# Scaling the softmax rows on DVE instead of ACT, and putting the transposes first in a group of attention's PE work

## The chip, the cores and the metric

The kernel runs on one core of a Trainium2 chip. The metric is the time of one execution in device microseconds (us); the time before is the median of three runs, and the change is judged against it. The engines are PE (TensorE: matmuls, and the transposes that are made of matmuls), DVE (VectorE), ACT (ScalarE), POOL (GpSimd) and SP (SyncE, which here only issues transfers).

## The reference

```python
# q, k, v: (8 batches, 8 heads, 576 rows, 64)
scores = q @ k.T / 8 + slope[h] * -(i - j)       # only 0 <= i - j < 128, else -1e9
attn   = softmax(scores)                         # sum + 1e-9 in the denominator
x      = (attn @ v) -> (4608 tokens, 512)
h      = max(x @ w1, x @ w2, x @ w3)             # 512 -> 768
out    = h @ w_out                               # 768 -> 512
```

Attention has a causal window of 128, so a block of 128 query rows needs only its own and the preceding block of 128 keys. 576 rows are four blocks of 128 and one of 64.

## The kernel before, in words

**Attention** goes by tasks (batch, pair of heads): 32 tasks of five blocks, 160 steps in all. One step is one block of both heads.

- `products` computes scores for two steps at a time into PSUM (`ps_s`, or `ps_m` in batch 0), with 64x64 tiles of PE.
- `score` merges the two key blocks into one by a predicated copy (L329, L332), adds the bias and takes the maximum on DVE (L344), and takes the exponential on ACT (L348). The result is the tile `p`, 128 rows by two heads by 128, and a row sum in `st`.
- `sums_of` adds 1e-9 and takes the reciprocal on DVE (L357, L360), for two steps or one.
- `normalise` multiplies `p` by that reciprocal, one value per row: L367, once for each step and head, 320 times in all.
- `turn` transposes `p` for two steps on PE (L376, four transposes into the tile `pt`), copies `pt` to SBUF on ACT (L380, L386, L389), and POOL cuts it into the two triangles of the window (L390, L394), the tile `pp`.
- `mix` multiplies `pp` by `v` (L416) into `ps_x`, with column tiles of 64; the last block has 64x64 tiles. ACT copies the finished `ps_x` to `xk` (L425).

**The three-way maximum and the output product** are split into high and low parts (L442 on ACT, L443 on DVE) and multiplied in 128x128x288 matmuls with three products for each pair of parts. Batch 0 uses the plain weights (`plain_unit`, L585); batches 1 to 7 use a seven-product scheme on 2x2 blocks (`unit`, L623). The results are taken from three PSUM buffers (`ps_m0` to `ps_m2`) by DVE and ACT (`put`, L533 to L552, and L632).

**Weights** are made during batch 0 (L132 to L176: fetched by SP, decoded on ACT and DVE, split) and recombined during batch 1 (`add`, `add_part`, L183 to L205). From batch 2 on they are streamed from DRAM by transfers that POOL issues (L270), into a ring of two buffers.

**What sets the order.** `at(when, ...)` enters each piece of work with a time in steps; the list is sorted, and so the program order comes about. Attention of step s enters at s (shifted by 2 and 4 steps from batch 1 and 2 on); the matmul units are spread evenly between the ends of the attention of successive batches. So PE's work alternates: a run of 128x128x288 matmuls, and then a group of attention's work. Such a group is entered at one even step c: mix at c + 0.001, products at c + 0.002, turn at c + 0.003 (turn belongs to the pair that began four steps earlier, mix to the pair six steps earlier). A scheduler at compile time sets the fixed order of each engine's queue; from batch 2's seventh step on PE keeps the program order as written (`keep_in_program_order`).

Each engine takes its instructions strictly in its queue's order. An instruction of DVE that has to wait holds up all behind it.

Of the kernel before, what the change touches and what calls it, by code (L numbers as in the profile page):

```python
# [12 lines left out]
AF = mybir.ActivationFunctionType  # L13
ALU = mybir.AluOpType
# [4 lines left out]
LAG_T, LAG_X = 4, 6  # L19
# [10 lines left out]
def attention_maxout_kernel(  # L30
# [11 lines left out]
    nc = tc.nc  # L42
# [7 lines left out]
    NB = (S + P - 1) // P  # L50
# [35 lines left out]
        out=prev, in_=prev, pattern=[[1, P]], compare_op=ALU.is_gt, fill=0.0,  # L86
# [275 lines left out]
    def normalise(t, i):  # L362
        n = rows[i]
        st, two = stats[t, i // 2]
        for a, p in enumerate(two):
            for j in range(2):
                nc.scalar.activation(p[:n, j], p[:n, j], AF.Copy, scale=st[:n, 2, a, j:j + 1])  # L367

    def turn(s):
        pt = ps_t.tile([P, 2, 2, P], F32, name="pt")  # L370
# [270 lines left out]
    def at(when, what, *args):  # L641
        events.append((when, len(events), what, args))
# [3 lines left out]
    for t, (b, hp) in enumerate(tasks):  # L646
        for i in range(NB):
            s = t * NB + i + shift[b]
            if i == LOAD_I and t + 2 < len(tasks):
                at(s - 0.4, load, t + 2)  # L650
            if i == NB - 1 and t + 1 < len(tasks):
                at(s - 0.4, load_v, t + 1)
            if i == 0 and 0 < t < NP:
                at(s - 1, slopes, t)
            c = s - (t * NB + i) % 2

            if s == c:
                at(c + 0.002, products, t * NB + i)
                at(c + LAG_T + 0.003, turn, t * NB + i)
            at(s + 0.04, score, t, i)  # L660
            if i % 2 or i + 1 == NB:
                at(s + 0.9, sums_of, t, i)
                at(s + 1.3, normalise, t, i)
            e = t * NB + next(min(e + 1, NB - 1) for e in GROUPS if e >= i)
            at(e - e % 2 + shift[b] + LAG_X + 0.001, mix, t, i)
# [78 lines left out]
```

## Time and profile before

| | |
|---|---|
| median of 3 runs (lowest to highest) | 802.09 us (800.0 to 804.02) |
| the profiled execution's own time | 799.82 us |
| its span, from first to last instruction | 797.7 us |
| PE busy | 759.2 us (95%) |
| DVE busy | 559.9 us (70%) |
| ACT busy | 531.3 us (67%) |
| POOL busy | 166.8 us (21%) |
| mean granted TensorE clock | 0.964 |

The span stands 2.1 us below its own execution's time, and this execution 2.3 us below the median.

How to read it: a span of an engine is busy or idle, and for idle time the profile names what ended it (its releaser). The trace falls into four stages. Until 75 us there is only the attention of batch 0, with the first part of the weights' preparation. From 75 to 160 us the plain products of batch 0 run beside the attention of batch 1. From 160 to 300 us batch 1 runs with the recombined weights being made, and from 300 to 700 us the same pattern repeats for the later batches. After 700 us there is no attention left.

### The profile page before, as it was taken

The page shows a single profiled execution, that of the slowest core. Times are in us where ns is not written, and L with a number is a line of the kernel's source. Part 1 is how long each engine was busy: PE and PEld are TensorE (multiplying, and loading weights), DVE is VectorE, ACT ScalarE, POOL GpSimd, SP SyncE. Part 2 cuts the span into 40 slices and gives each one's busy share as a digit, 9 for nine tenths or more (in the row PEclk, how much of TensorE's full clock was granted, in tenths as well). Part 3 has the DMA queues.
Part 4 walks back from the last instruction along what each step waited for, and adds up shares of the span by engine and source line. Part 5 has one row for each costly group of instructions (what it writes and reads, how often), then busy time and mean ns, then how long its engine had stood idle before and what let it go on. Part 6 is the DMA issues. An engine that isn't in the chain of part 4 may idle for free.

```text
span 797.7 us, 18112 instructions
## 1 busy us (share of the span) xinstructions
PE 759.2 (95%) x6344; PEld 674.2 (85%) x6344; DVE 559.9 (70%) x1897; ACT 531.3 (67%) x1736; POOL 166.8 (21%) x374
## 2 busy tenths in 40 slices
PE   4776998999999999999999999999999999999987
PEld 2434987998888998899989999898988999899987
DVE  5677888488999757793777747793777747673662
ACT  6888888568878656775667657676667667552332
POOL 1221111111214122221223122221222122201100
PEclk7756999999999999999999999999999999999999
DMA  8775785387899459864887459864788458755951
GB/s 282 266 243 171 228 302 208 115 297 231 318 329 314 166 196 320 286 215 138 285 295 252 162 187 323 282 234 136 277 285 257 160 195 288 245 198 195 301 181 60
DMA packets 53771, 187.96 MB, mean 236 GB/s; under 512 B 5936, under 2 KB 14896, under 8 KB 46768
## 3 DMA queue, kind: packets, MB, share of 16 engines
q0 software_dynamic: 15552, 99.10, 37.6%
q1 hardware_dynamic: 37984, 87.64, 32.0%
q8 instruction: 50, 0.82, 0.4%
q14 instruction: 41, 0.34, 0.1%
q10 hardware_dynamic: 144, 0.07, 0.0%
HBM read 154.53 MB, written 32.24 MB: 234 GB/s over the span
## 4 chain that ended last, share of the span: by engine, by line
PE 65%; DVE 12%; issue 9%; ACT 6%; DMA 4%; POOL 2%; SPq 0%; POOLq 0%; ACTq 0%; DVEq 0%
PE ps_m L623 44%; PE ps_x L416 6%; PE ps_m L585 6%; PE ps_s L314 5%; PE pt L376 4%; DMA wt<-keep 2%; ACT p L348 2%; DVE hs L443 2%; DVE xs L443 2%; DMA hs<-in_w_all 1%; DVE t L549 1%; DVE s L344 1%; DVE ps_s L332 1%; DVE hq L550 1%; ACT xs L442 1%
## 5 line engine op out<-in xcount | busy, mean ns | idle before, releaser
L623 PE MATMUL ps_m<-xs,wt 128*128 128x288 f32 x2646 | 370.4, 297 | 4.1 <-DMA wt<-keep 1.7
L623 PEld LDWEIGHTS ps_m<-xs,wt 128*128 128x128 f32 x2646 | 355.4, 188 | 7.9 <-DVE t L549 3.8
L390 POOL TENSOR_SCALAR_AFFINE_SELECT pp<-pr 128x256 f32<-128x256 f32 (+1 forms) x128 | 54.7, 428 | 401.9 <-ACT pr L389 220.2
L348 ACT ACTIVATE p<-s,st 128x128 f32<-128x128 f32 (+1 forms) x320 | 127.0, 399 | 16.0 <-DVE st L344 14.6
L632 ACT COPY t<-ps_m 128x288 f32<-128x288 f32 x231 | 89.7, 394 | 71.2 <-PE ps_m L623 70.8
L623 PE MATMUL ps_m<-hs,ow 128*128 128x288 f32 x882 | 124.0, 297 | 1.6 <-DVE hs L443 0.8
L367 ACT ACTIVATE p<-p,st 128x128 f32<-128x128 f32 (+1 forms) x320 | 110.5, 396 | 19.4 <-DVE st L360 19.4
L623 PEld LDWEIGHTS ps_m<-hs,ow 128*128 128x128 f32 x882 | 118.7, 188 | 3.1 <-ACT t L632 1.2
L270 POOL DMA_DIRECT2D wt<-keep x108 | 58.3, 539 | 194.3 <-PE ps_m L623 187.7
L344 DVE CUSTOM_DVE_ANT_0 s<-ps_s,bias 128x128 f32<-128x128 f32 (+1 forms) x300 | 76.7, 281 | 17.4 <-PE ps_s L314 13.6
L416 PE MATMUL ps_x<-pp,v 128*64 128x256 f32 (+3 forms) x768 | 81.3, 339 | 3.7 <-POOL pp L390 3.6
L332 DVE COPY_PREDICATED ps_s<-prev,ps_s 128x256 f32<-128x256 uint8 x120 | 50.8, 423 | 46.2 <-PE ps_s L314 44.7
L549 DVE TENSOR_TENSOR t<-ps_m,t 128x288 f32<-128x288 f32 x126 | 56.5, 452 | 36.3 <-PE ps_m L623 24.2
L314 PE MATMUL ps_s<-qk 64*64 64x192 f32 (+1 forms) x1080 | 70.2, 336 | 9.2 <-DVE st L344 5.0
L416 PEld LDWEIGHTS ps_x<-pp,v 128*64 128x64 f32 (+1 forms) x768 | 46.1, 142 | 29.9 <-issue 10.6
L442 ACT CAST hs<-hq 128x288 fp32r<-128x288 f32 x117 | 49.0, 430 | 31.9 <-DVE hq L550 16.5
L376 PE MATMUL pt<-ident,p 128*128 128x128 f32 (+1 forms) x320 | 59.2, 296 | 11.2 <-ACT p L367 7.1
L376 PEld LDWEIGHTS pt<-ident,p 128*128 128x128 f32 (+1 forms) x320 | 34.8, 146 | 40.3 <-issue 18.9
L585 PE MATMUL ps_m<-xs,wt 128*128 128x288 f32 x432 | 63.3, 306 | 3.3 <-DVE xs L443 2.6
L585 PEld LDWEIGHTS ps_m<-xs,wt 128*128 128x128 f32 x432 | 60.6, 196 | 4.2 <-DVE xs L443 3.0
L314 PEld LDWEIGHTS ps_s<-qk 64*64 64x64 f32 x1080 | 41.1, 138 | 26.7 <-issue 10.5
L389 ACT COPY pr<-pt 128x256 f32<-128x256 f32 x64 | 18.9, 321 | 66.5 <-PE pt L376 66.5
(58 smaller groups left out, 849.4 us busy)
## 6 DMA issues: line engine op xcount, KB each, us to landing
wt<-keep POOLq DMA_DIRECT2D x54, 1024.0 KB, 7.3
wt<-keep POOLq DMA_DIRECT2D x54, 768.0 KB, 5.5
qk<-in_qk SPq DMA_DIRECT2D x31, 576.0 KB, 5.8
hs<-in_w_all SPq DMA_DIRECT2D x24, 512.0 KB, 5.0
v<-in_v SPq DMA_DIRECT2D x32, 320.0 KB, 4.6
keep<-wt SPq DMA_DIRECT2D x36, 256.0 KB, 3.8
outT<-t SPq DMA_DIRECT2D x64, 144.0 KB, 1.8
wt<-keep SPq DMA_DIRECT2D x27, 256.0 KB, 4.2
```

Of the source, the lines that this page charges most:

```text
L270: nc.gpsimd.dma_start(wts[n, a], keep[n % 9][a])
L314: pe(nc.tensor.matmul(ps[j][d:d + D, o:o + k1 - k0], lhsT=qkt[t][j * D:(j + 1) * D, 0, q0:q0 + D], rhs=qkt[t][j * D:(j + 1) * D, 1, k0:k1] ...
L332: nc.vector.copy_predicated(both[:, :, P:], mask.unsqueeze(1).broadcast_to([n, 2, P]), both[:, :, :P],)
L344: nc.vector.tensor_tensor_reduce(out=s[:n], in0=ps[j][:n, P:2 * P], in1=(bias if i else bias0)[:n, 2 * hp + j, :], scale=-0.125, scalar=3. ...
L348: nc.scalar.activation(p[:n, j], s[:n], AF.Exp, bias=st[:n, 0, a, j:j + 1], scale=-1.0, accum_out=st[:n, 1, a, j:j + 1])
L367: nc.scalar.activation(p[:n, j], p[:n, j], AF.Copy, scale=st[:n, 2, a, j:j + 1])
L376: pe(nc.tensor.transpose(out=pt[:, a, j, :n], in_=p[:n, j], identity=ident[:n, :n]))
L416: pe(nc.tensor.matmul(x[j * D:(j + 1) * D, c:c + e - a], lhsT=vv[:n, i, j * D:(j + 1) * D], rhs=w[:n, j].rearrange("p a b -> p (a b)")[:, ...
L549: nc.vector.tensor_tensor(out=s, in0=ps, in1=e, op=ALU.add)
L585: pe(nc.tensor.matmul(ps, lhsT=lt, rhs=rt, start=m == 0 and c == 0, stop=m == len(pairs) - 1, skip_group_check=True,))
L623: pe(nc.tensor.matmul(ps, lhsT=lt, rhs=rt, start=i == 0 and k in (0, 1, 4), stop=i == len(pairs) - 1, skip_group_check=True,))
L632: nc.scalar.copy(out=e, in_=ps)
```

## The change

Two edits. `normalise` issues its multiplication as a DVE `tensor_scalar` with the reciprocal as a per-partition scalar, where it was an ACT `activation` with `Copy` and that scale. And `turn` is entered at c + 0.000 where it was at c + 0.003, so that it stands ahead of mix and products of the same group.

```diff
@@ normalise
         for a, p in enumerate(two):
             for j in range(2):
-                nc.scalar.activation(p[:n, j], p[:n, j], AF.Copy, scale=st[:n, 2, a, j:j + 1])
+                nc.vector.tensor_scalar(
+                    out=p[:n, j], in0=p[:n, j], scalar1=st[:n, 2, a, j:j + 1], scalar2=None, op0=ALU.mult
+                )
@@ the list of events
             if s == c:
                 at(c + 0.002, products, t * NB + i)
-                at(c + LAG_T + 0.003, turn, t * NB + i)
+                at(c + LAG_T, turn, t * NB + i)
```

Lines of the changed kernel from L368 on have numbers two higher (transposes L378, mix L418, splits L444 and L445, units L625).

What that does to the queues, at three places. The first is PE's queue in the repeating pattern of the later batches; `pt` is written by transposes, `ps_s` by score products, `ps_x` by mix, `ps_m` by the 288-wide matmuls. Before:

```order
L623 MATMUL ps_m_5883<-xs,wt_5729 128x288 x6
L416 MATMUL ps_x<-pp,v 64x256 x4
L314 MATMUL ps_s<-qk 64x192 x6
L376 MATMUL pt<-ident,p 128x64 x2
L376 MATMUL pt<-ident,p 128x128 x2
L623 MATMUL ps_m_5955<-xs,wt_5792 128x288 x6
```

And with the change:

```order
L625 MATMUL ps_m_5883<-xs,wt_5729 128x288 x6
L378 MATMUL pt<-ident,p 128x64 x2
L378 MATMUL pt<-ident,p 128x128 x2
L418 MATMUL ps_x<-pp,v 64x256 x4
L314 MATMUL ps_s<-qk 64x192 x6
L625 MATMUL ps_m_5955<-xs,wt_5792 128x288 x6
```

The transposes moved from the end of the group to its beginning; the 288-wide matmuls now come directly after the score products.

The second is DVE's queue in batch 1, at about 230 us of the trace (`hs_3317` are recombined weights, `hq` the running maximum that is read from the PSUM buffers `ps_m`). Before:

```order
L443 TENSOR_TENSOR hs<-hq,hs 128x288
L195 TENSOR_TENSOR hs_3317<-hs_3316 128x256 x2
L195 TENSOR_TENSOR hs_3317<-hs_3317,hs_3316 128x256
L552 TENSOR_TENSOR hq<-ps_m_3265,t 128x288
L195 TENSOR_TENSOR hs_3317<-hs_3316,hs_3317 128x256
L552 TENSOR_TENSOR hq<-ps_m_3336,t 128x288
```

And with the change:

```order
L445 TENSOR_TENSOR hs<-hq,hs 128x288
L367 TENSOR_SCALAR p<-p,st 128x128 x4
L195 TENSOR_TENSOR hs_3317<-hs_3316 128x256 x2
L195 TENSOR_TENSOR hs_3317<-hs_3317,hs_3316 128x256
L554 TENSOR_TENSOR hq<-ps_m_3265,t 128x288
L195 TENSOR_TENSOR hs_3317<-hs_3316,hs_3317 128x256
L554 TENSOR_TENSOR hq<-ps_m_3336,t 128x288
```

Four multiplications now stand ahead of the reads that free PE's PSUM buffers.

The third is ACT's queue towards the end of batch 0's attention. `xk_783` is the second half of the attention's result for batch 0 (`xk_796` in the changed program), `xk_456` the first (`xk_469`); `xs` are the split parts that the first 288-wide matmuls multiply. Before, both casts of the first half follow the last copy into the second:

```order
L152 CAST ow_119<-hs_697 128x256
L425 COPY xk_783<-ps_x 128x576
L442 CAST xs<-xk_456 128x576 x2
L348 ACTIVATE p,st<-s,st 128x128 x2
L442 CAST xs<-xk_783 128x576 x2
```

With the change the casts of the first half stand much earlier, before any copy into the second:

```order
L427 COPY xk_469<-ps_x 128x576
L444 CAST xs<-xk_469 128x576
L348 ACTIVATE p,st<-s,st 128x128 x2
L444 CAST xs<-xk_469 128x576
L388 COPY pp<-pt 128x2x128
L391 COPY pr<-pt 128x256
L142 ACTIVATE hs_432<-hs_432 128x512
```

The first operands of the 288-wide matmuls are thus cast some forty rows of the queue ahead of the last part of the attention's result. POOL's queue is the same in both programs, row by row; on SP a few loads of `qk` and `v` change places with neighbouring transfers of weights.

## The prediction

> **What bounds the kernel now.** I read the page's totals first, then the busy time by stage, then what PE waits for inside the later stages. Totals:
>
> ```profile
> span 797.7 us, 18112 instructions
> PE 759.2 (95%) x6344; PEld 674.2 (85%) x6344; DVE 559.9 (70%) x1897; ACT 531.3 (67%) x1736; POOL 166.8 (21%) x374
> PEclk7756999999999999999999999999999999999999
> ```
>
> By stage (columns: stretch, its length, busy time of PE, weight loads, DVE, ACT, POOL with their instructions, granted clock, DMA share, GB/s):
>
> ```profile
> 0.00:75.00 75.00, 48.78 (x313) 24.57 (x313) 50.47 (x200) 61.46 (x205) 15.11 (x42) 0.68 0.74 247
> 75.00:140.00 65.00, 61.93 (x517) 55.49 (x517) 54.28 (x171) 55.70 (x167) 10.43 (x22) 0.95 0.70 239
> 160.00:300.00 140.00, 138.90 (x1218) 125.96 (x1217) 115.79 (x399) 104.10 (x344) 28.91 (x57) 1.00 0.79 266
> 300.00:700.00 400.00, 398.79 (x3464) 361.48 (x3463) 277.33 (x972) 267.02 (x905) 99.99 (x226) 1.00 0.72 241
> ```
>
> From 300 to 700 us PE stands idle for 1.2 us of 400. Nothing that ACT or DVE does less can shorten that stage by more; only PE's own work counts there, and how long PE takes to get from one kind of matmul to the next. Before 75 us it is otherwise: PE is busy 48.78 of 75 us at a granted clock of 0.68, and ACT is the fullest engine. The waits of PE between 140 and 700 us (engine, tile, line, waited for: total, times, longest) confirm the first half of this:
>
> ```profile
> PE ps_m L623 <- DVE t L549: 1.0, 5, 0.2
> PE ps_m L623 <- ACT t L632: 0.6, 1, 0.6
> PE ps_m L623 <- DVE wt L153: 0.4, 1, 0.4
> ```
>
> No transposes appear: in these stages PE never waits for a scaled p. ACT's multiplication is far ahead of its use, and taking it off ACT removes no wait of PE there. What the change can win lies ahead of 140 us; what it can lose lies in PE's order everywhere, and on DVE.
>
> **What one multiplication costs on DVE.** The trace has no fp32 multiplication by a per-partition scalar on DVE. The nearest rows (busy, mean ns):
>
> ```profile
> L344 DVE CUSTOM_DVE_ANT_0 s<-ps_s,bias 128x128 f32<-128x128 f32 x240 | 61.9, 283 | 16.6 <-PE ps_s L314 13.6 <-ACT p L348 1.4
> L357 DVE TENSOR_SCALAR st<-st 128x4 f32<-128x4 f32 x64 | 13.1, 204 | 17.7 <-ACT p L348 16.7
> L143 DVE TENSOR_SCALAR hs<-hs 128x512 int32<-128x512 int32 x24 | 10.4, 432 | 0.2
> ...
> 39.21 0.28 DVE L344 CUSTOM_DVE_ANT_0 s<-ps_s,bias 128x128 f32<-128x128 f32 x1
> 39.42 0.07 DVE L344 DVE_READ_ACCUMULATOR2_ANT st<- 128x1 f32 x1
> ```
>
> The same instruction takes 204 ns over 4 elements and 432 ns over 512; on the line between, 128 elements take 204 + 124 x 228/508 = 260 ns. The last two rows show that the next instruction starts 0.07 us before a record ends (39.21 to 39.42 for a record of 0.28), so that one multiplication holds DVE for about 0.19 us. Bounds: 0.13 us (L357's 204 ns less 0.07, no price per element) and 0.28 us (L344's whole record). ACT's side is read directly, by stretch (ACT busy and instructions of L367):
>
> ```profile
> 10.40:74.90 64.50, 13.07 (x40) 0.63 0.73 242
> 190.00:270.00 80.00, 12.19 (x36) 1.00 0.87 302
> sum 689.60, ACT 110.52; mean ACT 27.63
> ```
>
> So ACT loses 110.5 us and DVE gains 320 x 0.19 = 61 us. The multiplication adds no wait to DVE's queue: it follows L357 and L360, which have waited for the same exponentials there. PE's transposes wait for DVE instead of ACT.
>
> **Term 1, the first 75 us: minus 3 us.** The same stretches for all engines:
>
> ```profile
> 10.40:74.90 64.50, 44.87 (x269) 22.22 (x269) 47.64 (x187) 57.29 (x191) 12.81 (x32) 0.63 0.73 242
> 190.00:270.00 80.00, 79.03 (x698) 71.58 (x698) 77.23 (x269) 65.90 (x217) 19.43 (x36) 1.00 0.87 302
> 270.00:300.00 30.00, 30.00 (x260) 27.05 (x259) 15.03 (x58) 17.24 (x65) 5.88 (x15) 1.00 0.54 182
> ```
>
> ACT works 57.29 of 64.5 us, 89%, in a loop that runs through PE, DVE, ACT and POOL. It falls to 57.3 - 13.1 = 44.2 us, but DVE rises to 47.6 + 40 x 0.19 = 55.2 us and becomes the fullest. If the loop fills its fullest engine to 89% again, the stretch takes 55.2 / 0.89 = 62 us, 2.5 us less. Filled to 97% as DVE is from 190 to 270 us (77.23 of 80), it would take 57 us, minus 7.5; at 82%, 67 us, plus 3. Behind it, the first 288-wide matmul waits for its operand, and soon after ACT waits for weights:
>
> ```profile
> 74.89 0.53 PE L585 MATMUL ps_m<-xs,wt 128*128 128x288 f32 x2 [2.59 <-DVE xs L443]
> ...
> ACT hs L138 <- DMA hs<-in_w_all: 5.1, 4, 2.1
> ```
>
> In the new queues the casts of the first half stand some forty rows earlier, so the 2.59 us should go too. But the second row (75 to 145 us) shows ACT held by transfers in the plain stage, and PE cannot use a lead that the weights do not share. I count minus 5 from both, give back 2 there, and take minus 3, with minus 8 and plus 3 as ends.
>
> **Term 2, PE's order: plus 3.5 us.** A group of attention's work between 288-wide matmuls, taken apart (start, length, count), and the median record of each kind (min/median/max ns):
>
> ```profile
> 443.52 0.56 PE L623 MATMUL ps_m<-hs,ow 128*128 128x288 f32 x3
> 444.01 0.88 PE L314 MATMUL ps_s<-qk 64*64 64x192 f32 x16
> 444.82 0.66 PE L376 MATMUL pt<-ident,p 128*128 128x128 f32 x4
> 445.24 0.64 PE L623 MATMUL ps_m<-hs,ow 128*128 128x288 f32 x3
> ...
> L623 PE MATMUL ps_m<-hs,ow x882: 288/295/406, 255.7 to 793.9; 128*128 128x288 f32 x177
> L376 PE MATMUL pt<-ident,p x320: 221/273/477, 14.6 to 696.2; 128*128 128x128 f32 x128, 64*128 64x64 f32 x32
> ```
>
> The last start in a row is its start plus length less one record. Ahead of the group, the last wide matmul starts at 443.52 + 0.56 - 0.295 = 443.79: 0.22 to the first score product. From there to the first transpose 0.81, to the first wide matmul 0.42, to the second 0.22 (three starts in 0.64 - 0.295 = 0.345, the last two 0.13 apart). Sum 1.67 us. The new order has edges that the trace shows elsewhere at full clock:
>
> ```profile
> 29.61 0.44 PE L376 MATMUL pt<-ident,p 128*128 128x128 f32 x2
> 29.97 0.39 PE L314 MATMUL ps_s<-qk 64*64 64x192 f32 x4
> ...
> 161.23 0.49 PE L314 MATMUL ps_s<-qk 64*64 64x192 f32 x6
> 161.66 0.53 PE L585 MATMUL ps_m<-hs,ow 128*128 128x288 f32 x2
> ```
>
> From the last transpose (29.61 + 0.44 - 0.27 = 29.78) to the first score product 0.20. From the last score product to a wide matmul 0.25, as long as to a transpose in the old order (a record of 0.32 ends the 0.49, so it starts at 161.40), and from that matmul to the second 0.53 - 0.295 = 0.24. What the trace never has is a transpose directly after a wide matmul. The reverse costs nothing to speak of (four transposes, then the wide matmul, in 0.42), so I put the wide one at its own 0.13 and three further transposes at 0.11. The new group: 0.13 + 3 x 0.11 + 0.20 + the scores' 0.56 + 0.25 + 0.24 = 1.71 to 1.72 us, 0.05 more than 1.67. Mix, where it is in the group, stands between the same neighbours but one, and its entry costs what the scores' does. In groups with the 64-row block a switch of shape inside the transposes goes or comes; these about cancel. The count:
>
> ```profile
> 75.00:700.00 625.00, 47.68 (x280) 29.02 (x280) 0.99 0.72 242
> ```
>
> 280 transposes are 70 groups: 70 x 0.05 = 3.5 us, all on PE's path. Ends: minus 4, if a transpose starts in the shadow of the wide matmul ahead of it and its 0.11 vanishes for half of them; plus 13, if that edge costs what the entry into the scores does, 0.22 instead of 0.13, and its second start comes late as well (0.14 more a group).
>
> **Term 3, DVE from 190 to 270 us: plus 3 us.** There DVE is at 77.23 of 80 us, while PE stands for only 0.97. Another 36 x 0.19 = 6.8 us makes 84 us of work in 80. Its queue holds the reads of PE's three PSUM buffers behind four multiplications each time, so that DVE's lateness becomes PE's. Against it: from 270 us DVE has 15 of 30 us free, and weights split ahead of their use can be late. I take 3 of the 4 us of excess; ends 0 and 36 x 0.28 = 10 less the 2.8 us free, 7. Later stages have room: 277.33 of 400 us and some 174 x 0.19 = 33 more.
>
> Transposes come earlier in their group by mix and scores, 2 us at most; behind them ACT's copies and POOL's cuts get that much more time. POOL's queue is unchanged, and its idle time is not on the path. SP's exchanged loads I cost at nothing: they change places with single transfers of a few us, while loads of q, k and v are issued more than a step ahead; without that cover each would delay one group by that time.
>
> **The sum.** -3 + 3.5 + 3 = +3.5 us. On the profiled 799.8 us that is 803.3; on the median, 2.3 us higher, 805.6, say 806. Its own range, from moving the three terms by about 3 us each, is 802 to 811.
>
> **Rivals.**
>
> *It cancels (801).* If each change between array shapes on PE costs the same, term 2 is nothing: wide to narrow, narrow to narrow and narrow to wide occur as often in the new order, and the transposes have the wide shape. Then -3 + 3 - a little for DVE, about -1. For it: going from scores to a wide matmul takes 0.25 us, as to a transpose. Against it: the second start after the switch is later for the wide matmul (0.24 against its 0.13) than for a transpose (0.42 less 2 x 0.11 and 0.03 leaves 0.17 against 0.11). The Trainium skill, TensorEngine Tiling (Array Packing), section Tiling Modes, says that changing the tiling mode drains TensorE; by that rule, counted per switch, the order would be neutral. The trace agrees that each switch costs time, and shows that the costs are unequal.
>
> *Faster (797.5).* The first stage was bound by ACT and DVE fills up to 97%: minus 7.5 with the early casts' gain lost to the transfers, term 3 hidden in DVE's free time behind 270 us, term 2 as above: -7.5 + 3.5 = -4, or 798, and less if term 2 is smaller. For it: ACT at 89%; against it: DVE at 55 of 64.5 us is nearly as full as ACT was. It decides if DVE's mean record of the multiplication stays below 0.2 us.
>
> *Much slower (815).* A transpose behind a wide matmul is a switch: 70 x 0.14 = 10 us on top of the forecast. For it: nothing but that no row shows this edge; against it: its reverse is free.
>
> **How the numbers follow.** What this measurement can tell from no change is 0.5%, 4 us: faster is below 798.1, slower above 806.1. The forecast gets 0.42, half of it above 806.1; the cancelling 0.20; faster 0.20; much slower 0.18. That makes slower 0.21 + 0.18 = 0.39, rounded to 0.4; faster 0.15 of its case and 0.05 of the cancelling, 0.2; the same 0.4. The range, 796 to 817, takes in the faster and the much slower case and leaves out only the far ends.
>
> **What would show it.** In the changed profile: L367 on DVE at 0.2 to 0.28 us; the first 288-wide matmul before 72 us and without a wait for xs; groups such as that at 444 us longer by 0.05 us, and the period of a batch between 300 and 700 us by some 0.5 us; PE's idle time from 190 to 270 us at 3 us or more, put down to DVE. I am wrong if the first wide matmul starts later than now, if the period grows by 2 us, or if PE waits for transposes' operands at all.

## The result: slower by 0.5%, and where the time went

Over 20 executions of each kernel the median is 804.9 us after the change and 800.7 us before. The ratio is 1.005, with a 95% interval of 1.0032 to 1.0067: about 4 us slower. (The 802.09 us that the prediction starts from was the median of three of these.) The profiled execution of the changed kernel took 802.77 us against 799.82.

The totals of the changed kernel's page:

```profile
span 801.1 us, 18111 instructions
PE 760.7 (95%) x6344; PEld 673.4 (84%) x6344; DVE 614.7 (77%) x2217; ACT 449.5 (56%) x1416; POOL 183.2 (23%) x374
PEclk9777999999999999999999999999999999999999
```

DVE is 55 us busier and ACT 82 us less busy, and PE has the same work. The busy time by stage after the change (columns as in the prediction: length, PE, weight loads, DVE, ACT, POOL, clock, DMA share, GB/s):

```profile
0.00:75.00 75.00, 49.01 (x326) 25.39 (x327) 56.65 (x238) 52.85 (x166) 17.26 (x42) 0.80 0.76 252
75.00:140.00 65.00, 65.00 (x552) 57.43 (x552) 61.47 (x227) 49.54 (x145) 17.85 (x24) 1.00 0.73 249
140.00:190.00 50.00, 49.32 (x424) 45.19 (x421) 37.38 (x135) 27.93 (x89) 8.13 (x16) 1.00 0.65 213
190.00:270.00 80.00, 76.19 (x663) 67.59 (x662) 79.12 (x278) 52.83 (x163) 21.59 (x34) 1.00 0.81 279
300.00:700.00 400.00, 397.87 (x3440) 359.67 (x3438) 306.64 (x1143) 218.51 (x725) 103.35 (x226) 1.00 0.72 238
```

The counts in the second column show PE's progress. By 140 us the changed kernel has done 326 + 552 = 878 PE instructions, the kernel before 313 + 517 = 830: a lead. From 190 to 270 us it does 663 where the kernel before does 698: DVE stands at 79.12 of 80 us, PE's idle time is 3.81 us instead of 0.97, and the lead is spent. From 300 to 700 us it does 3440 instead of 3464.

To follow this more finely I compare the start of the n-th 288-wide matmul of both traces. There are 4104 in each program, so that the n-th stands at the same point of the matmuls' work (they are called wide matmuls below):

| 288-wide matmul | before, us | after, us | difference |
|---|---|---|---|
| first | 74.89 | 72.65 | -2.2 |
| 300th | 135.2 | 128.8 | -6.5 |
| 600th | 187.0 | 181.4 | -5.6 |
| 1200th | 298.1 | 297.4 | -0.7 |
| 3450th | 700.3 | 702.9 | +2.5 |
| last | 793.9 | 797.1 | +3.3 |

So: 6.5 us won ahead of 135 us, 5.8 lost between there and 300, 3.2 lost between 300 and 700, and 0.7 behind it. PE's waits after the change (engine, tile, line, waited for: total, times, longest), first for 190 to 270 us, then for 300 to 700 us:

```profile
PE ps_m L625 <- DVE wt L153: 2.2, 2, 1.4
PE ps_m L625 <- DVE hq L546: 0.6, 1, 0.6
PE pt L378 <- DVE p L367: 0.4, 1, 0.4
...
PE ps_m L625 <- DVE t L551: 1.1, 5, 0.2
PE ps_m L625 <- DVE hq L546: 1.0, 5, 0.2
```

In the full stretch PE waits above all for `wt`, the low part of the weights' split, which DVE makes (L153). Behind 300 us the second row is new: DVE takes a result out of PSUM late (L546), five times.

### The profile page after: what moved, and what is told of

Read it like the earlier page. It is cut to its first block, busy times and chain, and to the rows that moved or that the text cites. A ratio compares the mean times of both kernels' runs of the same rounds, so it can differ in the third digit from the quotient of the medians.

```text
span 801.1 us, 18111 instructions
## 1 busy us (share of the span) xinstructions
PE 760.7 (95%) x6344; PEld 673.4 (84%) x6344; DVE 614.7 (77%) x2217; ACT 449.5 (56%) x1416; POOL 183.2 (23%) x374
## 4 chain that ended last, share of the span: by engine, by line
PE 78%; DVE 8%; DMA 5%; issue 4%; ACT 2%; POOL 1%; SPq 1%; POOLq 0%; ACTq 0%; DVEq 0%
PE ps_m L625 50%; PE ps_m L587 9%; PE ps_x L418 8%; PE ps_s L314 6%; PE pt L378 5%; DMA wt<-keep 2%; DMA hs<-in_w_all 2%; DVE hs L445 1%; DVE t L551 1%; ACT p L348 1%; DVE s L344 1%; DVE hq L552 1%; DVE ps_s L332 1%; DMA hs<-w 1%; POOL wt L270 1%
## 5 line engine op out<-in xcount | busy, mean ns | idle before, releaser
L625 PE MATMUL ps_m<-xs,wt 128*128 128x288 f32 x2646 | 374.2, 298 | 9.0 <-DVE wt L153 2.2
L625 PEld LDWEIGHTS ps_m<-xs,wt 128*128 128x128 f32 x2646 | 355.4, 188 | 27.6 <-issue 10.4
L392 POOL TENSOR_SCALAR_AFFINE_SELECT pp<-pr 128x256 f32<-128x256 f32 (+1 forms) x128 | 71.2, 556 | 301.6 <-ACT pr L391 176.4
L625 PE MATMUL ps_m<-hs,ow 128*128 128x288 f32 x882 | 123.2, 297 | 1.4 <-DVE hs L445 0.8
L625 PEld LDWEIGHTS ps_m<-hs,ow 128*128 128x128 f32 x882 | 118.3, 188 | 4.2 <-DVE hs L445 1.2
L418 PE MATMUL ps_x<-pp,v 128*64 128x256 f32 (+3 forms) x768 | 84.2, 336 | 5.2 <-POOL pp L392 5.0
L367 DVE TENSOR_SCALAR p<-p,st 128x128 f32<-128x128 f32 (+1 forms) x320 | 77.6, 293 | 0.9
L418 PEld LDWEIGHTS ps_x<-pp,v 128*64 128x64 f32 (+1 forms) x768 | 46.8, 141 | 31.4 <-POOL pp L392 9.9
L444 ACT CAST hs<-hq 128x288 fp32r<-128x288 f32 x117 | 50.0, 435 | 33.2 <-DVE hq L552 23.2
L378 PE MATMUL pt<-ident,p 128*128 128x128 f32 (+1 forms) x320 | 56.6, 284 | 6.6 <-DVE p L367 5.6
L348 ACT ACTIVATION_READ_ACCUMULATOR p<-s,st 128x1 f32 (+1 forms) x320 | 60.4, 189 | 0.0
L445 DVE TENSOR_TENSOR hs<-hq,hs 128x288 fp32r<-128x288 f32 x117 | 53.5, 464 | 8.3 <-ACT hs L444 8.2
```

What stands on the lines that cost most here:

```text
L348: nc.scalar.activation(p[:n, j], s[:n], AF.Exp, bias=st[:n, 0, a, j:j + 1], scale=-1.0, accum_out=st[:n, 1, a, j:j + 1])
L367: nc.vector.tensor_scalar(out=p[:n, j], in0=p[:n, j], scalar1=st[:n, 2, a, j:j + 1], scalar2=None, op0=ALU.mult)
L378: pe(nc.tensor.transpose(out=pt[:, a, j, :n], in_=p[:n, j], identity=ident[:n, :n]))
L392: nc.gpsimd.affine_select(out=pp[t, i - 1][:, :, 1, :n], in_=r[:, a, :, :n], pattern=[[0, 2], [-1, n]], compare_op=ALU.is_gt, fill=0.0, ba ...
L418: pe(nc.tensor.matmul(x[j * D:(j + 1) * D, c:c + e - a], lhsT=vv[:n, i, j * D:(j + 1) * D], rhs=w[:n, j].rearrange("p a b -> p (a b)")[:, ...
L625: pe(nc.tensor.matmul(ps, lhsT=lt, rhs=rt, start=i == 0 and k in (0, 1, 4), stop=i == len(pairs) - 1, skip_group_check=True,))
```

## The experiments

All were timed in five rounds against the kernel before; each ratio has its 95% interval. The "ledger theory" of the expectations adds up the times that the traces show place by place, and takes it that these add.

### The kernel before against itself

This kernel was to hold only the new order, but its text was that of the kernel before. The expectation speaks of the kernel that was meant:

> Only the order is changed: transposes first in a group, while ACT keeps the multiplication. Ledger theory: in the changed kernel's trace the groups with four transposes and no 64-row block are 0.044 us longer than before, those with it 0.195 longer or 0.151 shorter, 0.037 on average; 70 groups make +2.6 us, a ratio of 1.003, and the first wide matmul stays near 75 us, with no lead at 135 us. Rival (the order costs nothing, all of the loss is DVE's): ratio 1.000.

Measured: 1.0012 (0.9988 to 1.0037), the comparison of one program with itself, so it says nothing on either theory. It is the gauge for what follows: differences of 0.1% are nothing.

### Only DVE's multiplication

The first edit of the change alone; the transposes stay last in their group.

> Only the engine is changed: DVE multiplies for all batches, transposes stay last in their group. Ledger theory: 4.2 us of the change less 2.6 for the order, +1.6 us, a ratio of 1.002, with the same lead of about 6 us at 135 us and the same loss of it between 150 and 245 us. Rival (the order costs nothing): the whole +4 us, 1.005.

Measured: 804.0 us, 1.0047 (1.0022 to 1.0073). The engine alone makes as much as the whole change, which is what the rival said, though not for its reason, as the order alone shows below. The lead is there (7.3 us at the 300th wide matmul) and gone at the 1200th (0.2 us). Waits of PE from 190 to 270 us, then DVE's queue around the longest of them:

```profile
PE ps_m L625 <- DVE st L344: 2.3, 1, 2.3
PE ps_m L625 <- DVE wt L153: 1.5, 2, 0.9
PE ps_m L625 <- DVE hq L546: 0.7, 1, 0.7
```

```profile
217.12 0.44 DVE L552 TENSOR_TENSOR hq<-t,hq 128x288 f32<-128x288 f32 x1
217.49 0.94 DVE L153 TENSOR_TENSOR wt<-hs,wt 128x768 fp32r<-128x768 f32 x1
218.36 0.44 DVE L551 TENSOR_TENSOR t<-ps_m,t 128x288 f32<-128x288 f32 x1
218.72 0.27 DVE L344 CUSTOM_DVE_ANT_0 s<-ps_s,bias 128x128 f32<-128x128 f32 x1
218.93 0.08 DVE L344 DVE_READ_ACCUMULATOR2_ANT st<- 128x1 f32 x1
218.93 0.44 DVE L552 TENSOR_TENSOR hq<-t,hq 128x288 f32<-128x288 f32 x1
```

No row has a wait in brackets, and each starts before the one ahead of it has ended: DVE works without a gap here, and PE waits until 219.60 us.

### DVE's multiplication in batches 0 and 1 only

```diff
-                nc.scalar.activation(p[:n, j], p[:n, j], AF.Copy, scale=st[:n, 2, a, j:j + 1])
+                if tasks[t][0] < 2:        # batch
+                    nc.vector.tensor_scalar(...)
+                else:
+                    nc.scalar.activation(...)
```

> DVE multiplies in batches 0 and 1 only (up to about 140 us), ACT in the six others, old order. Ledger theory: the lead of about 6 us at 135 us is real and nothing takes it back, as DVE's queue from 150 us on is the old one; -6 us, a ratio of 0.9925, with a lead still near 5 us at 270 us. Rival, ceiling theory: between 160 and 245 us DVE (97% busy before the change) and the weights' transfers set the pace whatever PE brings along, so that the lead is gone by 245 us in any case: ratio 0.998 to 1.000.

Measured: 795.3 us, 0.9943 (0.992 to 0.9967), faster than both kernels. In its trace the lead is 6.9 us at the 300th wide matmul, 5.2 at the 1200th and 5.3 at the last. The ceiling theory falls: nothing between 160 and 245 us takes the lead back by itself. The stretch from 190 to 270 us:

```profile
190.00:270.00 80.00, 78.85 (x699) 70.32 (x699) 72.61 (x246) 62.07 (x201) 18.74 (x34) 1.00 0.81 286
```

### DVE's multiplication from batch 2 on only

The same condition with `>= 2`.

> DVE multiplies from batch 2 on, ACT in batches 0 and 1, old order. Ledger theory: no lead, and DVE's extra work between 150 and 270 us delays PE all the same: 36 records of 0.28 us onto 77 of 80 busy us, +4 us there and +1 to 2 us later, a ratio of 1.006. Rival, ceiling theory (the loss in the changed kernel was only a lead given back): at most +2 us, 1.0025.

Measured: 806.3 us, 1.007 (1.0038 to 1.0103), as the ledger theory said and too much for its rival. Its trace falls behind by 6.9 us between the 300th and the 1200th wide matmul, without any lead to give back. PE's waits for DVE from 190 to 270 us are 4.5 us in all, against 0.4 before. The loss is thus DVE's added work in that stretch.

### DVE's multiplication in batch 0 only

> DVE multiplies in batch 0 alone, old order. Ledger theory: the lead of the two-batch kernel is made in two places; batch 0 gives the 2.5 to 3 us that it had at the 100th wide matmul, and PE's stall of 2.4 us near 129 us, behind ACT, stays: -3 us, a ratio of 0.9965. Rival (all of the lead comes from batch 0): -5 us, 0.994, as with both batches.

Measured: 796.8 us, 0.9958 (0.9937 to 0.9978). The interval holds both expectations; the trace decides. At the 300th wide matmul the lead is 6.2 us, as with both batches, so batch 0 makes it, and PE's stall near 129 us is gone though ACT still multiplies in batch 1. My reading of that stall, that ACT's load in batch 1 causes it, was wrong. The lead stands at 6.0 us at the 3450th wide matmul and is 2.4 at the last: behind 700 us, where nothing is multiplied on DVE, PE waits 4.0 us for streamed weights (1.7 before).

### DVE's multiplication everywhere but in batch 2

> DVE multiplies in all batches but the third (batch 2, 150 to 241 us), old order. Ledger theory: the lead of 5 to 6 us stands at 270 us, since DVE's queue in the full stretch is the old one, and from 300 us on the stalls cost the 3 us that the all-DVE trace shows there: -2.5 us, a ratio of 0.997. Rival (whatever is multiplied on DVE later costs as much, since the next batch takes the place of this one): 1.003 or more.

Measured: 796.4 us, 0.9952 (0.9931 to 0.9974). Against DVE in all batches (1.0047) the one batch of 40 multiplications is worth some 7.6 us. Its trace has a lead of 6.0 us at the 1200th wide matmul and 3.6 at the 3450th. The windows of this kernel:

```profile
190.00:270.00 80.00, 79.07 (x703) 70.64 (x703) 75.25 (x261) 57.71 (x187) 17.48 (x34) 1.00 0.82 286
300.00:700.00 400.00, 398.14 (x3436) 359.77 (x3436) 305.54 (x1130) 214.14 (x717) 100.57 (x224) 1.00 0.72 238
```

With DVE at 75.25 of 80 us, PE is at 79.07 and does 703 instructions; with DVE at 79.12 it was at 76.19 and did 663. Later batches, where DVE has a quarter of its time free, cost far less apiece.

### Only the order

```diff
-                at(c + LAG_T + 0.003, turn, t * NB + i)
+                at(c + LAG_T, turn, t * NB + i)
```

> Only the order is changed (transposes first in a group), ACT multiplies. The run labelled e1_order did not hold this edit: its kernel was the one of before, so that its ratio is that of the kernel with itself. Ledger theory: 70 groups longer by 0.035 us on average, as in the changed kernel's trace, +2.5 us and a ratio of 1.003, with +1.6 us between 300 and 700 us. Rival (the order is free, since DVE alone already gave 1.0047 of the 1.005): 1.000.

Measured: 805.8 us, 1.006 (1.0038 to 1.0081). The order alone costs 4.8 us, more than either theory gave. Its trace wins 3.5 us up to the 300th wide matmul, though ACT multiplies (PE's stall of 2.4 us near 129 us is 0.5 here), and loses 5.5 from there to the 1200th: from 190 to 270 us PE waits 3.1 us for reads of PSUM by DVE and ACT and for the weights' split, against 1.0 before. It loses 3.8 us from the 1200th to the 3450th, where the longer groups make at most 1.6 (nine of each of five kinds, by the lengths given under term 2), and 1.8 behind that. Waits of PE from 300 to 700 us:

```profile
PE ps_m L623 <- ACT t L632: 2.4, 4, 0.6
PE ps_m L623 <- DVE t L549: 1.1, 5, 0.2
```

The first row is in neither of the kernels that the change compares: one stall a batch behind ACT's copy of a result out of PSUM (the eviction of the expectations). I compare ACT's queue around it with the same place before. Before, where the first wide matmul behind the group starts at 345.7 us:

```profile
347.16 0.41 ACT L348 ACTIVATE p<-s,st 64x128 f32<-64x128 f32 x1
...
347.95 0.39 ACT L632 COPY t<-ps_m 128x288 f32<-128x288 f32 x1
348.23 0.44 ACT L442 CAST hs<-hq 128x288 fp32r<-128x288 f32 x1
348.56 0.40 ACT L632 COPY t<-ps_m 128x288 f32<-128x288 f32 x1
349.34 0.67 ACT L442 CAST xs<-xt 128x576 fp32r<-128x576 f32 x1 [0.38 <-DVE xt L446]
349.92 0.67 ACT L442 CAST xs<-xk 128x576 fp32r<-128x576 f32 x1
```

With the order alone, where that matmul starts at 347.9 us:

```profile
349.21 0.68 ACT L442 CAST xs<-xt 128x576 fp32r<-128x576 f32 x1 [0.45 <-DVE xt L446]
349.80 0.66 ACT L442 CAST xs<-xk 128x576 fp32r<-128x576 f32 x1
350.37 0.40 ACT L348 ACTIVATE p<-s,st 64x128 f32<-64x128 f32 x1
...
351.47 0.68 ACT L632 COPY t<-ps_m 128x288 f32<-128x288 f32 x2
```

Before, the exponentials and both copies stand ahead of the two casts of x; now the casts, 1.3 us together, stand ahead of them. The copy starts 3.6 us behind the matmul instead of 2.3, and PE waits for it. Nothing in the edit names these casts: the order of ACT's queue follows from the order in which the pieces are written.

### The order, with DVE multiplying in batches 0 and 1

> DVE multiplies in batches 0 and 1, ACT in the others, and the order is the new one in all. Ledger theory: the two add up, 0.9943 + 0.003 = 0.997, because PE is the bound from 270 us on and every longer group is paid in full. Rival (the order is free): 0.9943.

Measured: 803.8 us, 1.0035 (1.0017 to 1.0053). On top of the 0.9943 the new order costs 0.9%, about 7 us, so the rival (that it is free) falls, and the sum is exceeded too. Between the 600th and the 1200th wide matmul this trace loses 4.2 us, and the one without the new order 0.7.

### The order from batch 3 on only

```diff
+                at(c + LAG_T + (0.0 if b >= 3 else 0.003), turn, t * NB + i)
```

> The new order (transposes first) from batch 3 on only, the old one in batches 0 to 2; ACT multiplies throughout. Theory of two costs: the trace of the order alone shows 3.8 us between 300 and 700 us, of it 2.5 in PE's stalls behind ACT's eviction (four of 0.7 us among them) and the rest in longer groups; these come back here in full, with some 10 of the 70 groups fewer and nothing lost or won ahead of 245 us: +3.8 us, a ratio of 1.0045 to 1.005. Rival (the order costs nearly all of its time in the full stretch from 150 to 270 us, and later only the 50 groups by 0.035 us): +1.7 us, 1.002 or less.

Measured: 805.5 us, 1.0052 (1.0029 to 1.0075). The trace loses 3.7 us from the 1200th to the 3450th wide matmul, and PE's waits in that stage hold the same row as with the order everywhere:

```profile
PE ps_m L623 <- ACT t L632: 2.3, 4, 0.6
PE ps_m L623 <- DVE t L549: 1.2, 5, 0.2
```

The order's cost lies mainly in the later batches; in the first ones, by the trace of the order alone, it wins 3.5 us and loses 5.5. By the gaps between the starts of wide matmuls the longer groups make 1.6 of the 3.7 us and four stalls of 0.73 us make 2.9; elsewhere PE gains 0.8.

### Two other orders

Attention products, transposes, scores (`LAG_T + 0.0015`):

> Order within a group is attention products, transposes, scores (before: attention products, scores, transposes; changed: transposes, attention products, scores); ACT multiplies. So the scores are last, as in the changed order, but the transposes do not follow a wide matmul where attention products are there. Theory of late scores: what the order alone costs beyond its longer groups (about 2 of 4.8 us) comes from scores that end a group, since exponentials and the evictions queued behind them on ACT wait for them. Then stalls of PE between 300 and 700 us behind ACT's eviction return as in the order alone (4 of up to 0.7 us), and the groups add their own: by the edges of the traces, entry 0.22, to a transpose 0.25, to the scores 0.20, to the wide matmuls 0.25 + 0.24, against 0.22 + 0.31 + 0.25 + 0.25 before, 0.13 us more in some 50 groups, together 1.010 to 1.015. Rival (early transposes are what hurts, by displacing ACT's work): no more than the longer groups, and no stall behind ACT's eviction, 1.008 or less.

Measured: 811.6 us, 1.0135 (1.0098 to 1.0172), the size forecast by the theory of late scores, but not for its reason: the stall behind ACT's copy does not come. The 22 groups with 16 attention products are 0.35 us longer than before (2.92 against 2.57), twelve others 0.19 and twelve 0.04. That makes 10.6 us, about the timed loss of 10.8. The trace does not bear out that the groups are all of it: its execution, 816.04 us, was the slowest of six, and loses 16.3 us between the 300th and the 3450th wide matmul, 6.2 of them between the 600th and the 900th, where PE waits 3.1 us for the weights' split (L153). A group of this kernel:

```profile
445.23 1.25 PE L416 MATMUL ps_x<-pp,v 128*64 128x256 f32 x16
446.41 0.66 PE L376 MATMUL pt<-ident,p 128*128 128x128 f32 x4
446.99 0.76 PE L314 MATMUL ps_s<-qk 64*64 64x192 f32 x12
447.68 2.68 PE L623 MATMUL ps_m<-hs,ow 128*128 128x288 f32 x18
```

Going from the last attention product to a transpose takes 0.31 us where its columns are 256, and 0.15 where they are 64; that edge is what this order adds.

Scores, attention products, transposes (`products` at c + 0.0005), with ACT multiplying, and with DVE in batches 0 and 1:

> Order within a group is scores, attention products, transposes; ACT multiplies. Theory of late scores: exponentials start 0.4 to 0.6 us earlier in most groups and nothing is queued later; groups as long as before within 0.05 us; ratio 0.997 to 1.000, ACT's time of waiting for the scores' row minima at or below the 8 us that it has before between 300 and 700 us. Rival (any exchange in the tuned order costs, whatever is first): 1.003 to 1.006 as with the changed order.

> DVE multiplies in batches 0 and 1, ACT in the others, with the order scores, attention products, transposes. If both parts add: 0.9943 times the ratio of the order alone, 0.991 to 0.994. Rival (any exchange in the order costs as the changed one did on top of this engine choice, 0.009): 1.003.

Measured: 1.0079 (1.0048 to 1.0111) and 1.0063 (1.0033 to 1.0094). The profiled executions, 802.11 and 801.73 us, lie some 5 us below their medians, so the traces do not show the whole loss. The theory of late scores fails here as a forecast of the time. With ACT multiplying PE waits only 0.2 us in all from 300 to 700 us, less than in any kernel above, and the stalls saved pay for groups that are up to 0.15 us longer: the stage takes what it took before. But between the 600th and the 900th wide matmul 6.9 us are lost (4.2 with DVE in batches 0 and 1), at the weights' split again, this time with ACT's cast of it named first (190 to 270 us, ACT multiplying):

```profile
PE ps_m L623 <- ACT wt L152: 3.2, 2, 2.8
PE ps_m L623 <- DVE wt L153: 1.6, 2, 0.9
```

The rival, that any exchange in this order costs, stands for the three other orders that were run; I would not make a rule of it.

## Why the prediction was right, and where it was not

**The total was right**: +3.5 us forecast, +4.2 measured between the medians, 806 against 804.9. (The 806 stood on a base of 802.09, which twenty executions put at 800.7.) That it came so near was luck: two of its terms were half of what they should have been, with opposite signs, and the third was right in one half only.

**Term 1, the first 75 us (-3; ends -8 and +3): the sign right, one half of the mechanism wrong.** The lead is 6.5 us at the 300th wide matmul. The term was minus 2.5 for a faster loop, minus 2.5 for the casts that come earlier, and 2 given back. The faster loop did not come: the last score products of batch 0 end at 72.30 us before (first row) and at 72.19 after (second row), and DVE, now the fullest engine, is filled to 84% ahead of the first wide matmul (52.10 of 62.25 us), not to 89. The casts came nearly as forecast: the first wide matmul waits 0.46 and 0.17 us for xs instead of 2.59, and starts at 72.65 us, not before 72:

```profile
71.01 1.29 PE L314 MATMUL ps_s<-qk 64*64 64x192 f32 x14
...
71.31 0.88 PE L314 MATMUL ps_s<-qk 64*64 64x192 f32 x16 [0.39 <-DVE st L344]
72.65 1.06 PE L587 MATMUL ps_m<-xs,wt 128*128 128x288 f32 x6 [0.46 <-DVE xs L445]
73.88 4.38 PE L587 MATMUL ps_m<-xs,wt 128*128 128x288 f32 x31 [0.17 <-DVE xs L445]
```

A wait for xs of 2.6 to 2.9 us stands in every trace in which ACT multiplies in batch 0; where DVE does, it is at most 1.1.

What failed as well is the step "give back 2 there". The lead does not shrink behind the first wide matmul, it jumps from 2.5 us at the 276th to 6.5 at the 290th. The trace before has a stall there, which I took to be the transfers' doing, and the granted clock is 0.50 in the 3.4 us behind it (130.0 to 133.4); after the change neither comes:

```profile
129.35 0.99 PE L314 MATMUL ps_s<-qk 64*64 64x192 f32 x16 [2.39 <-DVE st L344]
```

That jump is not DVE's alone: it is 3.1 to 4.0 us in every kernel that has either edit in its first batches, 3.4 with the order alone, and 2.0 or less in those that start as the kernel before does. What removes the stall is thus not isolated. The runs with DVE in batches 0 and 1, and in batch 0 alone, show that the lead is real and kept when nothing else is changed: 0.9943 and 0.9958.

**The multiplication's price (0.19 us of DVE) was right.** The record is longer than the 260 ns that I had put between the nearest rows, the time that it holds DVE is not: from one of these to what follows without a gap it takes 0.196 us, median of 297.

```profile
L367 DVE TENSOR_SCALAR p<-p,st x320: 265/281/444, 14.5 to 692.0; 128x128 f32<-128x128 f32 x128, 64x128 f32<-64x128 f32 x32
```

For ACT I left the same overlap out: "ACT loses 110.5 us" adds up whole records, and ACT is 82 us less busy. No term rested on it, since DVE is the fullest engine of the first stage either way.

**Term 3, DVE from 190 to 270 us (+3; ends 0 and 7): right in mechanism, too small.** The loss between the 300th and 1200th wide matmul is 5.8 us, of which 19 longer groups, at the 0.035 us given below, explain 0.7. The place, DVE's share and the 3.81 us of PE's idle time came as forecast, and DVE from batch 2 on, without a lead, loses 6.9 us there. What failed is the step "84 us of work in 80", with 3 taken for the excess of 4: the excess over the stretch is not all that a full queue costs. PE's waits come one by one inside it: 2.4 of the 5.8 us are waits for the split weights (DVE 2.2, ACT 0.2), the others are single waits of at most 0.8 us, for PSUM buffers, a scaled p and a transfer. That time lost at one of them is not made up at the next, and that this is the whole of the difference, is argued, not shown.

**Term 2, PE's order (+3.5): the edges right, the reason for the time mostly another.** A group of the kind shown in the prediction is 0.045 us longer, against 0.05: the transposes in front start 0.133 us behind a wide matmul, where I had put 0.13.

```profile
444.78 0.60 PE L378 MATMUL pt<-ident,p 128*128 128x128 f32 x4
445.30 0.88 PE L314 MATMUL ps_s<-qk 64*64 64x192 f32 x16
446.12 4.10 PE L625 MATMUL ps_m<-hs,ow 128*128 128x288 f32 x29
```

Of the groups with the 64-row block half are 0.195 us longer and half 0.151 shorter, where I had written "these about cancel". Over the 58 groups of the five common kinds the mean is 0.035 us, 2.4 us for 70. But what I left out is that an order on PE is also an order on ACT and DVE: with ACT multiplying, a stall a batch comes behind ACT's copies, and the order alone costs 4.8 us. In the changed kernel ACT has lost that work and the row is missing; there DVE's late reads of PSUM stand in its place (L546, 1.0 us). From 300 to 700 us the forecast was 0.5 us a batch; it is 3.2 us over 4.46 batches, 0.7. The term's lower end was misreckoned: half of 70 x 0.11 us taken from 3.5 leaves about zero, not minus 4.

**The parts do not add.** Engine alone 1.0047, order alone 1.006, together 1.005. With DVE multiplying everywhere the order is nearly free (1.005 against 1.0047, about as far apart as a program is from itself); with ACT multiplying from batch 2 on it costs 0.6 to 0.9%. That ACT's eviction stalls go when ACT is relieved is shown by the rows; that both costs fall on the same waits for the split weights in batch 2, so that the second finds them already paid, is what the traces suggest and no run isolates. The stall near 129 us goes with either edit and can be won only once, which makes the overlap of the losses larger still.

**The rivals.** "It cancels" is excluded by the total, which it put about 1 us below the kernel before; its step that the order is free fails where ACT multiplies and nearly holds where DVE does. Its premise that each switch costs the same fails by the 0.31 and 0.20 us below. The Trainium skill, TensorEngine Tiling (Array Packing), section Tiling Modes, says that a change of tiling mode drains TensorE; the traces agree that such changes cost time (0.15 to 0.31 us from start to start), but not that counting them suffices. "Much slower" had as its only ground the unknown edge, which costs 0.133 us and is no switch. "Faster" had the size of the early gain (7.5 us) more nearly right than the forecast, but by luck, for the loop that was to give it gave nothing; and it failed because term 3 was not hidden in DVE's free time behind 270 us. Its condition, a mean record below 0.2 us, was the wrong measure: the record is 0.29 us, but a gain of that size came all the same.

**A point that I had excluded.** A wait of PE for a transpose's operand came, 0.4 us at 235 us, where DVE is full. The claim that the scaled p is always far ahead holds for the later batches only. As a sign of being wrong, "if PE waits for transposes' operands at all" was of no use: in the first 75 us PE waited 7.1 us for them before, and 5.2 after.

**Open.** Why the order of ACT's and DVE's queues in batch 2 is so sensitive that three different edits of PE's order all lose time there, with waits for the weights' split of 0.9, 3.1 and 4.8 us; a kernel that splits these weights earlier wasn't tried.

## What to carry to other kernels

Moving work from a fuller engine to a less full one has to be weighed stage by stage: here the same instruction won about 5 us in the two first batches, cost some 7 us in the one where DVE was already at 97%, and little per batch behind it, so the best kernel (0.9943) moves it only where it wins. Where the order of one engine's work is written by hand, a change there reorders the other engines' queues too; look in their timelines for what now stands ahead of the instruction that frees PSUM. A total that comes out right shows nothing of its terms: only the position of the same instruction in both traces, stage by stage, does.

## What was not expected of the hardware

**An edge between matmul shapes has a price that depends on both sides.** From start to start at full clock, and so with the first one's own time in it, by the traces of the kernel before, of the changed one and of scores last: wide matmul to a 128-column transpose 0.13 us, as to another wide one; wide to a 64-column transpose 0.22, as to scores or attention products; transpose to scores or attention products 0.20; scores to transposes 0.25; attention products of 256 columns to scores or to transposes 0.31.

**A stall of PE was mostly followed by a halved clock.** Behind 100 us the traces hold eight single stalls of PE of 2.2 to 2.9 us; seven of them are followed by 3.4 us at a granted clock of 0.50, in which wide matmuls start 0.24 us apart instead of 0.13. One stall of 2.3 us (DVE from batch 2 on) is not. Such a stall thus costs more than its length.

**The first 75 us vary from trace to trace, and the granted clock with them.** The kernel with the new order from batch 3 on starts as the kernel before does, and its first wide matmul came at 77.2 us against 74.9:

```profile
L585 PE MATMUL ps_m<-xs,wt x432: 288/295/606, 77.2 to 162.9; 128*128 128x288 f32 x144
```

Its granted clock up to 75 us was 0.57 against 0.68. Over all kernels in which ACT multiplies in the first batches it was 0.57 to 0.77, with DVE there 0.73 to 0.84. Whether the clock makes the lead or follows from it isn't settled by these runs; two executions of the kernel before with a recorded mean of 1.000 took 801.0 and 800.9 us, no less than the others (medians 800.5 and 801.9), which speaks against the first. One profile is thus worth no more than about 3 us in this stage, and the kept lead was judged by the timed ratios.
